# Wider rows for the loads of an attention block: V in rows of four keys with its middle keys copied on GpSimd, K in one load, output weights in row pairs

## The chip, the cores and the metric

The kernel runs on one core of a Trainium2 chip. The metric is the device time of one execution in microseconds (us). The core has a matrix engine (TensorE, "PE" in the profile, with its weight loads as "PEld"), VectorE ("DVE"), ScalarE ("ACT"), GpSimd ("POOL"), and SyncE ("SP"), which issues the DMA transfers; 16 DMA engines carry them.

## What is computed

```python
B, Sq, D = 8, 112, 640          # x:       [B, Sq, D]
H, Sk, Dh = 32, 512, 192        # k_cache, v_cache: [B, H, Sk, Dh]; wq: [D, H*Dh]; wo: [H*Dh, D]

def reference(x, k_cache, v_cache, wq, wo):
    q = (x @ wq).reshape(B, Sq, H, Dh).transpose(0, 2, 1, 3)
    scores = jnp.einsum("bhqd,bhkd->bhqk", q, k_cache) * (Dh ** -0.5)
    p = softmax(scores, axis=-1)
    o = jnp.einsum("bhqk,bhkd->bhqd", p, v_cache)
    return o.transpose(0, 2, 1, 3).reshape(B, Sq, H * Dh) @ wo
```

All inputs and the output are bf16. K and V are 50 MB each, and every byte of them is read once.

## The kernel before

**Units.** The 32 heads are cut into 8 groups of 4, and a unit is one group for one batch: 64 units, u = 8 g + b. A unit loads K and V of its four heads (768 KB each), computes the transposed scores, exponentiates them, multiplies by V, normalises, transposes the result and leaves it in `oT`. For each group, the projection of all queries (`do_Q`) and the output product (`do_O`) run as items of 128 rows or columns, handed out one to two of each per unit by the table `items_at`.

**TensorE** follows one written order (lines 883 to 893): scores of unit u (`do_S`, L840, 96 matmuls of 32 rows, four side by side), then PV of unit u-1 (`do_PV`, L856, 16 matmuls), then Q items (L803) and O items (L821) with the six transposes of unit u-1 (`do_T`, L868) between them. Group 0's queries are made before the loop from weights as they lie in memory (L810); groups 1 to 7 use weights that GpSimd has put into another order.

**Softmax sums.** No maximum is subtracted. The denominators come out of the PV product itself: each V tile has a column of ones before its first key and after its last (`vs`, columns 31 and 32 + 2 x 192 of each half), and a product reads 193 columns, one key's 192 and the ones column beside it. With four keys t = 0 to 3 in a partition the even ones read from the left, the odd ones to the right, so that a one is next to each key. Before the change each of the two halves of a tile holds two keys, with ones on both sides. The sums land in column 0 and column 193 of the product, `do_NM` on VectorE adds the two (L981) and takes the reciprocal (L984), and VectorE (L987) and ScalarE (L928) scale two heads each.

**VectorE** also turns K: `do_KT` (L976) transposes the loaded tile `kr` in 32x32 blocks of 4-byte pairs, four pieces a unit, five to eight pieces ahead of the scores. ScalarE does the exponentials (L921) and carries the queries (L913) and the transposed outputs (L938) out of PSUM.

**GpSimd** works in order, unit by unit: where the table `at` says so it reorders one 128-row piece of the next but one group's W_q (`reorder`, L1064, two copies), then it waits for the reciprocals of unit u and counts values out of range (L1079, L1080, L1082). VectorE's L980 waits for that count with a distance of three units. Ahead of the loop stand the five reorders for group 1.

**Loads.** SyncE issues all transfers from one list (from L1126), each after its own wait: K of unit u when the transposes of unit u-3 are done (`NK = 3` buffers), V of unit u when PV of unit u-4 is done (`NV = 4`), pieces of W_q when GpSimd has emptied the buffer, pieces of W_o when the group before last has been used. In the loop over u the order is K of u, V of u-1, then at most two pieces of W_q and two of W_o. K comes in two halves of 3,072-byte rows, V in two halves of 768-byte rows (two keys), W_o in pieces of 128 rows of 1,280 bytes, W_q in pieces of 1,536-byte rows. A window on the bytes in flight is in the code, but set so high that it never waits.

Of the kernel before, what the change touches and what calls it, by code (L numbers as in the profile page):

```python
# [6 lines left out]
BF16 = mybir.dt.bfloat16  # L7
F32 = mybir.dt.float32
I32 = mybir.dt.int32
# [657 lines left out]
def build_main(nc, x, k_cache, v_cache, wq, wo, out, flag):  # L667
    B, SQ, D = x.shape
# [9 lines left out]
    scale = float(DH) ** -0.5  # L678
    LO, HI = 2.0 ** -30, 2.0 ** 40
    NK, NV, NT = 3, 4, 3  # L680
    PW = 448
    RW = DH + 2
    WINDOW = 10 ** 9
    EARLY = 0
    PRE = 12
    EARLY_LOADS = ("k1", "q", "v0", "k2", "v1", "k3", "o", "v2")
    QN = (2, 2, 2)
# [26 lines left out]
    with ExitStack() as es:  # L714
# [9 lines left out]
        wqr = sb("wqr", [128, DC, 4 * DH], BF16)  # L724
        wos = sb("wos", [128, 2, 6, D], BF16)
        kr = [sb(f"kr{j}", [128, 16, DH], BF16) for j in range(NK)]
        vs = [sb(f"vs{j}", [128, 4, 2, PW], BF16) for j in range(NV)]
        kt = [sb(f"kt{j}", [128, 4, 3, 128, 2], BF16) for j in range(NT)]
        qT = [sb(f"qT{j}", [128, 6, R], BF16) for j in range(2)]
        pT = [sb(f"pT{j}", [128, 4, 4, 128], BF16) for j in range(2)]  # L730
# [18 lines left out]
        aX, aEX, aQ, aT, aNM = (sem(n) for n in ("aX", "aEX", "aQ", "aT", "aNM"))  # L749
        vI, vX, vKT, vSM, vRC, vNM, vO, vT = (sem(n) for n in ("vI", "vX", "vKT", "vSM", "vRC", "vNM", "vO", "vT"))  # L750
        gI0, gI, gB, gC, gV = (sem(n) for n in ("gI0", "gI", "gB", "gC", "gV"))
        gW = sem("gW")
        mX = [sem(f"mX{j}") for j in range(3)]
        mK = [[sem(f"mK{j}{h}") for h in range(2)] for j in range(NK)]
        mV = [[sem(f"mV{j}{h}") for h in range(2)] for j in range(NV)]
        mW0 = [sem(f"mW0{j}") for j in range(DC)]
        mWQ = [sem(f"mWQ{j}") for j in range(DC)]
        mWO = [[sem(f"mWO{j}{c}") for c in range(6)] for j in range(2)]
        mOUT = [sem(f"mOUT{j}") for j in range(MT)]
        XM = [(0, 2), (2, 4), (4, MT)]  # L760
        x_piece = [0, 0, 1, 1, 2, 2, 2]
# [20 lines left out]
        def _(pe):  # L782
# [31 lines left out]
            def do_O(it):  # L814
                _, g, m, h = it
                W(pe, aT, 8 * g + last_unit(m) + 1)
                bank_free(pe, it)
                for c in range(6):
                    if m == 0 and h == 0:
                        W(pe, mWO[g % 2][c], 16 * (g // 2 + 1))  # L820
                    mm = pe.matmul(ps[:, bank(it), 0:HO], oT[:, c, 128 * m:128 * (m + 1)],  # L821
                                   wos[:, g % 2, c, HO * h:HO * (h + 1)], start=(c == 0), stop=(c == 5))
                mm.then_inc(pO, 1)
# [20 lines left out]

            def do_PV(u):
                W(pe, aEX, 4 * (u + 1))
                for h in range(2):
                    W(pe, mV[u % NV][h], 16 * (u // NV + 1))
                W(pe, aT, u)
                W(pe, vNM, u)  # L850
                W(pe, aNM, u)
                for a in range(4):
                    for t in range(4):
                        k, e = divmod(a, 2)
                        o0, v0 = (0, 31) if t % 2 == 0 else (1, 32 + DH)
                        mm = pe.matmul(pv[:, k, e, o0:o0 + DH + 1], pT[u % 2][:, a, t, :],  # L856
                                       vs[u % NV][:, a, t // 2, v0:v0 + DH + 1], start=(t == 0), stop=(t == 3),
                                       skip_group_check=True)
                mm.then_inc(pPV, 1)

            def do_T(u):
                for j in range(6):
                    if j == 0:
                        W(pe, vNM, u + 1)
                    if j == 3:
                        W(pe, aNM, u + 1)
                    o0 = 2 * (RW * (j // 3) + 1) + SQ * (j % 3)
                    mm = pe.transpose(psb[:, 4, o0:o0 + SQ], os_[u % 2][:, 128 * j:128 * (j + 1)], ident[0:SQ, 0:SQ])  # L868
                mm.then_inc(pT_, 1)

            W(pe, gI, 1)
# [92 lines left out]
        def _(dve):  # L964
# [3 lines left out]

            def do_KT(u, t):
                if t == 0:  # L970
                    for h in range(2):
                        W(dve, mK[u % NK][h], 16 * (u // NK + 1))
                    W(dve, pS, 4 * (u - NT + 1))
                src = kr[u % NK][:, t:16:4, :].bitcast(I32).rearrange("p s (c i) -> p c s i", c=3)
                dst = kt[u % NT][:, t].rearrange("p c j e -> p c (j e)").bitcast(I32).rearrange("p c (j s) -> p c s j", s=4)
                dve.transpose(dst, src).then_inc(vKT, 1)  # L976
# [66 lines left out]
        @block.gpsimd  # L1043
        def _(gp):
            gp.memset(ident[:], 0.0).then_inc(gI0, 1)
            gp.wait_ge(gI0, 1)
            gp.affine_select(out=ident[:], in_=ident[:], compare_op=ALU.not_equal, fill=1.0, base=0,
                             pattern=[[-1, 128]], channel_multiplier=1).then_inc(gI, 1)
            for j in range(2):
                gp.memset(pT[j][:, :, :, SQ:128], 0.0)  # L1050
            for j in range(NV):
                gp.memset(vs[j][:, :, :, 31:32], 1.0)
                gp.memset(vs[j][:, :, :, 32 + 2 * DH:33 + 2 * DH], 1.0)
            gp.memset(cnt[:], 0.0).then_inc(gC, 1)
            gp.wait_ge(gC, 1)
            gp.memset(bad[:], 0.0).then_inc(gV, 1)
            gp.wait_ge(gV, 1)

            def reorder(g, dc):
                W(gp, mWQ[dc], 16 * g)  # L1060
                if dc == 0 and g >= 2:
                    W(gp, pQ, q_index[(g - 2, 5, 1)] + 1)
                for e in range(2):
                    ins = gp.tensor_copy(  # L1064
                        wqs[:, g % 2, dc, :].rearrange("p (k e a i) -> p e k a i", k=3, e=2, a=4)[:, e],
                        wqr[:, dc, :].rearrange("p (a k i e) -> p e k a i", a=4, k=3, e=2)[:, e])
                ins.then_inc(gW, 1)

            at = {}
            for g in range(1, NG):  # L1070
                for dc in range(DC):
                    at.setdefault(unit_of[(g - 2, 5, 1)] + 1 + dc if g >= 2 else -1, []).append((g, dc))
            for it in at.get(-1, []):
                reorder(*it)
            for u in range(NU):
                for it in at.get(u, []):
                    reorder(*it)
                W(gp, vRC, u + 1)
                gp.tensor_scalar(bad[:, 0, :], rinv[:, u % 4, :], LO, None, op0=ALU.is_lt)  # L1079
                gp.tensor_scalar(bad[:, 1, :], rinv[:, u % 4, :], HI, None, op0=ALU.is_gt).then_inc(gB, 1)  # L1080
                gp.wait_ge(gB, u + 1)
                gp.tensor_tensor(cnt[:], cnt[:], bad[:], op=ALU.add).then_inc(gC, 1)  # L1082
                gp.wait_ge(gC, u + 2)

        @block.sync
        def _(sp):
            loads = []

            def add(dst, src, s, count, waits):
                size = 2  # L1090
                for n in dst.shape:
                    size *= n
                loads.append((dst, src, s, count, waits, size))

            def load_x(j):
                m0, m1 = XM[j]
# [7 lines left out]
                else:  # L1104
                    add(wqr[:, dc, :], src, mWQ[dc], 16 * g, [(gW, DC * (g - 2) + dc + 1)])

            def load_wo(g, c):
                add(wos[:, g % 2, c, :], wo[4 * DH * g + 128 * c:4 * DH * g + 128 * (c + 1)], mWO[g % 2][c],
                    16 * (g // 2 + 1), [(pO, 2 * MT * (g - 1))])

            def load_k(u):
                g, b = divmod(u, B)
                src = k_cache[b, 4 * g:4 * g + 4].rearrange("a (j s) d -> (a j) (s d)", s=16)
                for h in range(2):
                    add(kr[u % NK][:].rearrange("p s d -> p (s d)")[:, 8 * DH * h:8 * DH * (h + 1)],
                        src[:, 8 * DH * h:8 * DH * (h + 1)], mK[u % NK][h], 16 * (u // NK + 1),
                        [(vKT, 4 * (u - NK + 1))])

            def load_v(u):
                g, b = divmod(u, B)  # L1120
                for h in range(2):
                    add(vs[u % NV][:, :, h, 32:32 + 2 * DH],
                        v_cache[b, 4 * g:4 * g + 4].rearrange("a (m h t) d -> h m a (t d)", h=2, t=2)[h],
                        mV[u % NV][h], 16 * (u // NV + 1), [(pPV, u - NV + 1)])

            load_x(0)  # L1126
# [5 lines left out]
            for step in EARLY_LOADS:  # L1132
# [3 lines left out]
                    for dc in range(DC):  # L1136
                        load_wq(1, dc)
                if step[0] == "o":
                    for c in range(6):
                        load_wo(0, c)  # L1140
            for u in range(4, NU + 1):
                if u < NU:
# [7 lines left out]
                for g in range(1, NG):  # L1150
                    d = u - (8 * g - 1)
                    if 0 <= d < 3:
                        load_wo(g, 2 * d)
                        load_wo(g, 2 * d + 1)
            total = 0
            ends = []
            for n, (dst, src, s, count, waits, size) in enumerate(loads):
                total += size
                ends.append(total)
                past = [i for i in range(n) if ends[i] <= total - WINDOW]  # L1160
                if past:
                    i = past[-1]
                    W(sp, loads[i][2], loads[i][3])
                for ws, wv in waits:
                    W(sp, ws, wv)
                sp.dma_start(dst, src).then_inc(s, 16)  # L1166
# [51 lines left out]
```

## Time and profile before

| | |
|---|---|
| median of 14 runs | 445.48 us (442.48 to 450.18) |
| the profiled execution | 444.12 us, of which the span from the first to the last instruction is 442.4 us |
| mean granted TensorE clock | 0.98 |
| busy: PE / DVE / ACT / POOL | 90% / 67% / 59% / 17% |
| DMA read and written | 117.5 MB and 1.15 MB, 268 GB/s over the span |
| K load, 384 KB, issue to landing | 128 of them, 5.3 us median |
| V load, 384 KB, issue to landing | 128 of them, 5.1 us median |
| W_o piece, 160 KB; W_q piece, 192 KB | 48 of them, 5.4 us; 35 of them, 5.6 us |

In the rows of the profile, a line such as "L976 DVE STREAM_TRANSPOSE kt<-kr 128x384 int32 ... x256 | 207.8, 867 | 8.4" gives the source line, the engine, the operation, what it writes and reads, the shape, how many there are, the busy time of all in us and the mean of one in ns, and after the second bar the time for which the engine stood idle just before them and what ended that. The row of a DMA queue gives packets, MB, and the share of 16 engines' span that its packets took. "Issue" is time in which an engine waited for nothing that the profile shows. The views with windows give the busy time of each engine in a stretch of time, the granted clock of TensorE, the share of the DMA engines and GB/s.

### The profile page before, as it was taken

Reading aid. Unit: us, or ns where it says so; the run is one execution under the profiler, and the core shown is the slowest. Engines: PE = TensorE matmul, PEld = TensorE weight load, DVE = VectorE, ACT = ScalarE, POOL = GpSimd, SP = SyncE. Lnnn points to the kernel's source line nnn. Section 1 sums busy time; section 2 is a strip of 40 time slices with the busy share of each in tenths; the row PEclk is TensorE's granted clock in tenths of the full one; section 3 lists DMA queues with packets and bytes.
Section 4 is the critical chain, followed back from the end, with each engine's and each line's share of the span. In section 5 each row is a group of like instructions: output and inputs, shape, how many; then the busy total and the mean of one; then the engine's idle time right before and its main releaser. Section 6 shows DMA issues by size and latency. Waiting matters only on the chain.

```text
span 442.4 us, 20613 instructions
## 1 busy us (share of the span) xinstructions
PE 397.7 (90%) x8948; PEld 299.2 (68%) x8948; DVE 297.6 (67%) x570; ACT 261.5 (59%) x549; POOL 76.8 (17%) x280
## 2 busy tenths in 40 slices
PE   7978999877999987999999899999789999988882
PEld 5556677655777765777776677777557777776661
DVE  1637877646777875877777568877648787788431
ACT  3557566644766755576665655676536766665440
POOL 1402222120122300222112201222001111111010
PEclk9989999989999999999999999999989999999898
DMA  8999999957989997799988799889857899897201
GB/s 266 368 362 337 361 362 314 310 192 221 323 257 313 313 354 224 233 286 339 337 281 257 253 347 295 246 260 319 287 162 225 257 333 314 267 309 232 73 33 37
DMA packets 100738, 120.10 MB, mean 271 GB/s; under 512 B 5664, under 2 KB 84256, under 8 KB 100640
## 3 DMA queue, kind: packets, MB, share of 16 engines
q1 hardware_dynamic: 100640, 118.71, 83.0%
q8 instruction: 72, 1.18, 1.1%
q14 instruction: 26, 0.21, 0.2%
HBM read 117.54 MB, written 1.15 MB: 268 GB/s over the span
## 4 chain that ended last, share of the span: by engine, by line
PE 88%; issue 7%; DVE 2%; DMA 1%; SPq 1%; ACT 0%; DVEq 0%
PE ps L856 22%; PE ps L821 20%; PE ps L840 19%; PE ps L803 19%; PE ps L868 5%; PE ps L810 2%; DMA wqs<-in_wq_dram 1%; DVE os L987 1%; SPq L1166 1%; DVE rinv L984 0%; DVE sm L981 0%; PE ps L789 0%; ACT oT L938 0%; DVE xT L1005 0%; DVE xs L1000 0%
## 5 line engine op out<-in xcount | busy, mean ns | idle before, releaser
L976 DVE STREAM_TRANSPOSE kt<-kr 128x384 int32<-128x384 int32 x256 | 207.8, 867 | 8.4 <-DMA kr<-in_k_cache_dram 8.4
L921 ACT ACTIVATE pT<-ps 128x448 bf16<-128x448 f32 x256 | 118.7, 548 | 78.7 <-PE ps L840 78.7
L821 PE MATMUL ps<-wos,oT 128*128 128x320 bf16 x672 | 111.8, 303 | 2.9 <-issue 1.9
L856 PE MATMUL ps<-vs,pT 128*128 128x193 bf16 x1024 | 99.7, 249 | 14.1 <-issue 13.3
L840 PE MATMUL ps<-qT,kt 32*128 32x112 bf16 x6144 | 90.2, 209 | 11.8 <-issue 11.8
L840 PEld LDWEIGHTS ps<-qT,kt 32*128 32x128 bf16 x6144 | 78.2, 93 | 31.8 <-issue 29.8
L856 PEld LDWEIGHTS ps<-vs,pT 128*128 128x128 bf16 x1024 | 84.1, 98 | 21.6 <-issue 15.9
L803 PE MATMUL ps<-xT,wqs 128*128 128x448 bf16 x420 | 94.1, 359 | 0.0
L821 PEld LDWEIGHTS ps<-wos,oT 128*128 128x128 bf16 x672 | 63.5, 99 | 31.0 <-issue 3.9
L981 DVE TENSOR_REDUCE sm<-ps 112x4 f32<-112x8 f32 x64 | 10.7, 167 | 105.3 <-PE ps L856 105.3
L913 ACT ACTIVATE qT<-ps 128x448 bf16<-128x448 f32 x96 | 52.2, 545 | 32.6 <-PE ps L803 25.0
L1079 POOL TENSOR_SCALAR bad<-rinv 112x4 f32<-112x4 f32 x64 | 14.6, 228 | 297.2 <-DVE rinv L984 296.8
L938 ACT ACTIVATE oT<-ps 128x672 bf16<-128x672 bf16 x64 | 46.7, 730 | 32.3 <-PE ps L868 32.3
L928 ACT ACTIVATE os<-ps,rinv 112x192 bf16<-112x192 f32 x128 | 46.9, 418 | 23.8 <-DVE rinv L984 21.8
L803 PEld LDWEIGHTS ps<-xT,wqs 128*128 128x128 bf16 x420 | 40.8, 99 | 28.3 <-issue 2.8
L1000 DVE TENSOR_TENSOR acc<-ps,acc 128x320 f32<-128x320 f32 x84 | 41.0, 488 | 5.2 <-PE ps L821 5.1
L1064 POOL COPY wqs<-wqr 128x384 bf16<-128x384 bf16 x70 | 33.2, 507 | 47.2 <-DMA wqr<-in_wq_dram 45.6
L987 DVE TENSOR_TENSOR os<-ps,rinv 112x384 bf16<-112x384 f32 x64 | 35.7, 558 | 6.5
L868 PE MATMUL ps<-ident,os 112*128 112x112 bf16 x384 | 30.1, 214 | 4.9 <-DVE os L987 3.1
L868 PEld LDWEIGHTS ps<-ident,os 112*128 112x128 bf16 x384 | 24.9, 98 | 13.0 <-DVE os L987 5.6
L1080 POOL TENSOR_SCALAR bad<-rinv 112x4 f32<-112x4 f32 x64 | 14.5, 226 | 4.1 <-issue 0.2
L810 PE MATMUL ps<-xT,wqs 128*32 128x448 bf16 x240 | 12.4, 353 | 1.9 <-ACT xT L904 0.9
(32 smaller groups left out, 63.3 us busy)
## 6 DMA issues: line engine op xcount, KB each, us to landing
kr<-in_k_cache_dram SPq DMA_DIRECT2D x128, 384.0 KB, 5.3
vs<-in_v_cache_dram SPq DMA_DIRECT2D x128, 384.0 KB, 5.1
wos<-in_wo_dram SPq DMA_DIRECT2D x48, 160.0 KB, 5.4
wqr<-in_wq_dram SPq DMA_DIRECT2D x35, 192.0 KB, 5.6
out_dram<-xs SPq DMA_DIRECT2D x7, 160.0 KB, 1.8
wqs<-in_wq_dram SPq DMA_DIRECT2D x5, 192.0 KB, 4.7
xs<-in_x_dram SPq DMA_DIRECT2D x2, 320.0 KB, 3.2
xs<-in_x_dram SPq DMA_DIRECT2D x1, 480.0 KB, 7.0
```

The source lines that it names most:

```text
L803: mm = pe.matmul(ps[:, bank(it), 0:HQ], wqs[:, g % 2, dc, 128 * c:128 * (c + 1)], rhs, start=(dc == 0), stop=(dc == DC - 1))
L821: mm = pe.matmul(ps[:, bank(it), 0:HO], oT[:, c, 128 * m:128 * (m + 1)], wos[:, g % 2, c, HO * h:HO * (h + 1)], start=(c == 0), stop=(c == 5))
L840: mm = pe.matmul(ps[:, a, SQ * t:SQ * (t + 1)], kt[u % NT][p, t, c // 2, :, c % 2], qT[g % 2][p, c, SQ * b:SQ * (b + 1)], start=(c == 0), ...
L856: mm = pe.matmul(pv[:, k, e, o0:o0 + DH + 1], pT[u % 2][:, a, t, :], vs[u % NV][:, a, t // 2, v0:v0 + DH + 1], start=(t == 0), stop=(t == ...
L868: mm = pe.transpose(psb[:, 4, o0:o0 + SQ], os_[u % 2][:, 128 * j:128 * (j + 1)], ident[0:SQ, 0:SQ])
L913: act.activation(qT[g % 2][:, c, HQ * h:HQ * (h + 1)], ps[:, bank(it), 0:HQ], ACTF.Copy).then_inc(aQ, 1)
L921: act.activation(pT[u % 2][:, a, :, 0:SQ], ps[:, a, 0:4 * SQ].rearrange("p (t q) -> p t q", t=4), ACTF.Exp, scale=scale).then_inc(aEX, 1)
L928: ins = act.activation(os_[u % 2][:, DH * (2 + e):DH * (3 + e)], pv[0:SQ, 1, e, 1:1 + DH], ACTF.Copy, scale=rinv[:, u % 4, 2 + e:3 + e])
L938: act.activation(oT[:, :, SQ * b:SQ * (b + 1)].rearrange("p (k c) q -> p k c q", k=2), src.rearrange("p k (c q) -> p k c q", c=3), ACTF.Co ...
L976: dve.transpose(dst, src).then_inc(vKT, 1)
L987: dve.tensor_tensor(os_[u % 2][:, 0:2 * DH].rearrange("p (e d) -> p e d", e=2), pv[0:SQ, 0, :, 1:1 + DH], rinv[:, u % 4, 0:2][:, :, None]. ...
L1000: ins = dve.tensor_tensor(ob[:, m, cs] if g == NG - 1 else acc[:, m, cs], src, acc[:, m, cs], op=ALU.add)
```

## The change

V's buffer becomes one row of four keys per head and partition: `vs` is [128, 4, 832] with the four keys at columns 32 to 799, a one at column 31 and a one at column 800. The two loads of a unit now split the heads (two each) and not the keys; each row is 1,536 bytes. The middle two keys have no ones beside them any more. GpSimd copies them into a new tile `vm` (two buffers) that holds key 1, two ones and key 2 (`middle`: two copies of 128 x 4 x 96 32-bit words a unit). PV reads keys 0 and 3 from `vs` and keys 1 and 2 from `vm`, and waits for GpSimd's count instead of the two loads' semaphores. `middle(0)` stands ahead of the reorders for group 1, `middle(1)` behind them, and `middle(u + 2)` at the end of unit u on GpSimd.

K of a unit is one load of 768 KB with 6,144-byte rows. W_o comes in three pieces a group of 256 rows, two rows (2,560 bytes) to a partition; so that the products match, the transposes of the attention output take every second column (a step of 2 in the weights that TensorE loads), and the third of the six waits for ScalarE's half where the fourth did. The window's code is taken out.

```diff
-        vs = [sb(f"vs{j}", [128, 4, 2, PW], BF16) for j in range(NV)]
+        vs = [sb(f"vs{j}", [128, 4, VW], BF16) for j in range(NV)]
+        vm = [sb(f"vm{j}", [128, 4, MW], BF16) for j in range(NM)]
...
             def do_PV(u):
                 W(pe, aEX, 4 * (u + 1))
-                for h in range(2):
-                    W(pe, mV[u % NV][h], 16 * (u // NV + 1))
+                W(pe, gM, u + 1)
...
-                        o0, v0 = (0, 31) if t % 2 == 0 else (1, 32 + DH)
-                        mm = pe.matmul(pv[:, k, e, o0:o0 + DH + 1], pT[u % 2][:, a, t, :],
-                                       vs[u % NV][:, a, t // 2, v0:v0 + DH + 1], start=(t == 0), stop=(t == 3),
-                                       skip_group_check=True)
+                        o0, src, v0 = [(0, vs[u % NV], 31), (1, vm[u % NM], 0), (0, vm[u % NM], DH + 1),
+                                       (1, vs[u % NV], 32 + 3 * DH)][t]
+                        mm = pe.matmul(pv[:, k, e, o0:o0 + DH + 1], pT[u % 2][:, a, t, :], src[:, a, v0:v0 + DH + 1],
+                                       start=(t == 0), stop=(t == 3), skip_group_check=True)
...
-                    if j == 3:
+                    if j == 2:
                         W(pe, aNM, u + 1)
                     o0 = 2 * (RW * (j // 3) + 1) + SQ * (j % 3)
-                    mm = pe.transpose(psb[:, 4, o0:o0 + SQ], os_[u % 2][:, 128 * j:128 * (j + 1)], ident[0:SQ, 0:SQ])
+                    mm = pe.transpose(psb[:, 4, o0:o0 + SQ], os_[u % 2][:, 256 * (j // 2) + j % 2:256 * (j // 2) + j % 2 + 255:2], ident[0:SQ, 0:SQ])
...
+            def middle(u):
+                for h in range(2):
+                    W(gp, mV[u % NV][h], 16 * (u // NV + 1))
+                W(gp, pPV, u - NM + 1)
+                for h in range(2):
+                    ins = gp.tensor_copy(vm[u % NM][:, :, (DH + 2) * h:(DH + 2) * h + DH].bitcast(I32),
+                                         vs[u % NV][:, :, 32 + DH * (1 + h):32 + DH * (2 + h)].bitcast(I32))
+                ins.then_inc(gM, 1)
...
+            middle(0)
             for it in at.get(-1, []):
                 reorder(*it)
+            for u in range(1, NM):
+                middle(u)
             for u in range(NU):
...
                 gp.wait_ge(gC, u + 2)
+                if u + NM < NU:
+                    middle(u + NM)
...
-            def load_wo(g, c):
-                add(wos[:, g % 2, c, :], wo[4 * DH * g + 128 * c:4 * DH * g + 128 * (c + 1)], mWO[g % 2][c],
+            def load_wo(g, k):
+                r0 = 4 * DH * g + 256 * k
+                add(wos[:, g % 2, 2 * k:2 * k + 2, :], wo[r0:r0 + 256].rearrange("(p e) d -> p e d", e=2), mWO[g % 2][k],
                     16 * (g // 2 + 1), [(pO, 2 * MT * (g - 1))])
...
-                for h in range(2):
-                    add(kr[u % NK][:].rearrange("p s d -> p (s d)")[:, 8 * DH * h:8 * DH * (h + 1)],
-                        src[:, 8 * DH * h:8 * DH * (h + 1)], mK[u % NK][h], 16 * (u // NK + 1),
-                        [(vKT, 4 * (u - NK + 1))])
+                add(kr[u % NK][:].rearrange("p s d -> p (s d)"),
+                    k_cache[b, 4 * g:4 * g + 4].rearrange("a (j s) d -> (a j) (s d)", s=16), mK[u % NK], 16 * (u // NK + 1),
+                    [(vKT, 4 * (u - NK + 1))])
...
                 for h in range(2):
-                    add(vs[u % NV][:, :, h, 32:32 + 2 * DH],
-                        v_cache[b, 4 * g:4 * g + 4].rearrange("a (m h t) d -> h m a (t d)", h=2, t=2)[h],
+                    add(vs[u % NV][:, 2 * h:2 * h + 2, 32:32 + 4 * DH],
+                        v_cache[b, 4 * g + 2 * h:4 * g + 2 * h + 2].rearrange("a (m t) d -> m a (t d)", t=4),
                         mV[u % NV][h], 16 * (u // NV + 1), [(pPV, u - NV + 1)])
```

## The prediction

> **What bounds the kernel now.** I read the page's busy shares first, then the chain that ended last, then the list of waits, and last the trace's own records of DMA packets around the places where TensorE stands still.
>
> ```profile
> PE 397.7 (90%) x8948; PEld 299.2 (68%) x8948; DVE 297.6 (67%) x570; ACT 261.5 (59%) x549; POOL 76.8 (17%) x280
> q1 hardware_dynamic: 100640, 118.71, 83.0%
> q8 instruction: 72, 1.18, 1.1%
> PE 88%; issue 7%; DVE 2%; DMA 1%; SPq 1%; ACT 0%; DVEq 0%
> ```
>
> TensorE is the bound: 88% of the chain is matmuls, none of which the change adds or removes. The DMA engines come next, 83.0% of 442.4 us = 367.3 us each. The only sizeable idle on the chain is "issue", 7% or 31 us: TensorE waits for nothing that the profile names. The list of waits of TensorE says where:
>
> ```profile
> PE ps L856 <- issue: 13.3, 9, 2.5
> PE ps L840 <- issue: 11.8, 11, 2.5
> PE ps L868 <- DVE os L987: 3.1, 7, 1.1
> ```
>
> No line names a V or K transfer: V, K and weights are in time, so a faster load pays nothing directly. But the "issue" gaps have a pattern. Number TensorE's instructions in order: every long gap lies at 193 plus a multiple of 256, and 256 instructions are one 16,384-byte packet of the instruction queue (the q8 row: 72 packets, 1.18 MB). Of 71 such crossings 26 have a gap, 30.1 us in all, and in each the refill packet started late: on average 3.8 us after the crossing before. Once it started, the next page was usable some 2.45 us later (packet at 25.46 us, TensorE on again at 27.96; at 243.01 and 245.46). The worst cases are crossings just before a V load: at 238.06 us a page began, V and a piece of W_q were issued at 238.61 to 239.59, their packets ran until about 243.0, and only then did the refill start. So **TensorE waits for its own instructions, and these wait behind the data**. A long gap costs twice, because the granted clock falls in the next 3.4 us:
>
> ```profile
> core 0: us, PE busy (x) PEld busy (x) DVE busy (x) ACT busy (x) POOL busy (x), PEclk, DMA share, GB/s
> 25.03:28.44 3.41, 0.86 (x60) 0.63 (x48) 0.00 (x0) 0.10 (x1) 0.00 (x0) 1.00 1.08 354
> 28.44:31.85 3.41, 3.41 (x25) 2.75 (x20) 0.51 (x3) 2.02 (x5) 0.00 (x0) 0.50 1.07 365
> 318.60:322.00 3.40, 0.94 (x12) 0.79 (x10) 0.57 (x1) 1.73 (x4) 0.00 (x0) 1.00 0.79 281
> 322.00:325.40 3.40, 3.40 (x16) 1.88 (x14) 1.68 (x4) 1.28 (x3) 0.65 (x3) 0.50 0.34 86
> ```
>
> Four such windows lie inside the work (from 28.4, 96.7, 322.0 and 414.2 us), each worth 1.7 us.
>
> A rule speaks against all this: the Trainium skill, "Runtime: NRT & Kernel Launch", Instruction fetch mechanics, says that crossing a 16 KiB boundary costs one step of a queue's tail and is mostly hidden. By it faster data would be worth nothing and the sum below would be zero. The trace decides: 26 of 71 crossings are not hidden.
>
> **The change, part by part.**
>
> *Rows of the loads.* Mean times of one packet in the trace's records: 768 B 40.9 ns (65,536 of them, all V), 1,280 B 59.9, 1,536 B 73.1 (W_q), 3,072 B 140.1 (16,384, all K), a semaphore write 9 ns; times their counts and over 16 engines they give the 367.3 us. After the change V is 32,768 rows of 1,536 B: 2,680 - 32,768 x 73.1 ns = 285 us less. K is 8,192 rows of 6,144 B, a size not in the trace: on the slope from 1,536 to 3,072 B (67.0 ns for 1,536 B more) it takes 140.1 + 2 x 67.0 = 274 ns, so 2,295 - 2,245 = 50 us less (nothing, if such a row is cut in two). W_o, 3,072 rows of 2,560 B at 118 ns for 6,144 at 59.9: 6 us less. 88 DMAs fewer save 1,408 semaphore writes, 13 us. Sum 354 us, over 16 engines **22.1 us, 6.0% of the DMA work**; the queue's share goes from 83% to about 78%. The Trainium skill, "DMA: Bandwidth & Descriptors", Why small descriptors are slow, gives about 3 cycles a packet beside one per 32 bytes: V's 2 x 27 cycles become 51, 5.6% of V's 167.5 us, 9.3 us, where the rows give 17.8. I take the rows; by the rule the 22.1 would be about 12.
>
> What it buys on the path: a refill that waits for data waits for 6% less of it. 26 crossings x 3.8 us x 6% = **-6.0 us** (-3.3 by the rule; 0 at the other end, if the wait is not made of data). One of the four half-clock windows, 1.7 us, may go with a gap that becomes shorter: half a chance, **-0.8 us**.
>
> *The copies on GpSimd.* Per unit two copies 128x384 int32. The nearest row is the reorder of W_q on the same engine, of as many elements:
>
> ```profile
> L1064 POOL COPY wqs<-wqr 128x384 bf16<-128x384 bf16 x70 | 33.2, 507 | 47.2 <-DMA wqr<-in_wq_dram 45.6
> ```
>
> 128 x 507 ns = 65 us, POOL at 142 us (32%). What hides it is depth: the copy for unit u+2 is made after the check of unit u, about 2 us after PV of unit u began to be normalised, and PV of u+2 comes two units, some 11 us, later. V of u+2 was issued when PV of u-2 ended and landed within 5.1 us (median). Behind it on POOL stands only the next unit's reorder, whose reader on TensorE is units away, and the check, which VectorE's L980 waits for three units later. A copy would have to take over 4 us to be seen. Nor does it hinder VectorE: its transposes (L976) that met a copy of L1064 took 876 ns, the others 865.
>
> *The start* is the exception. The copy for unit 0 stands ahead of the five reorders for group 1 and waits for V of unit 0:
>
> ```profile
> 15.20 4.56 POOL L1064 COPY wqs<-wqr 128x384 bf16<-128x384 bf16 x10 [12.72 <-DMA wqr<-in_wq_dram]
> 22.34 2.06 PE L803 MATMUL ps<-xT,wqs 128*128 128x448 bf16 x10
> 27.96 0.57 PE L840 MATMUL ps<-qT,kt 32*128 32x112 bf16 x30 [2.55 <-issue]
> ```
>
> V of unit 0 landed at 19.6 us; with shorter loads ahead say 19.1. Two copies, then 4.56 us of reorders: done at 24.7 instead of 19.8, and the Q products that began at 22.34 need them: TensorE waits 2.4 us. But 3.0 us of work later (27.7) it reaches the page end where it now waits until 27.96 for a refill asked for at 21.59, before the new wait. The new wait takes the old one's place: **0**. Without that cover it costs 2.4 us.
>
> *Queues and waits.* PV waits for one count of POOL instead of two of DMA: at most an instruction less. SP issues 88 DMAs fewer; K's second half was issued 0.4 us after the first and VectorE waited for both, so one load changes nothing there. A single K load leaves no gap for a refill to slip between halves: 0.4 us of each unit's 6, times half a K load (0.9 us), 0.06 us a page, 1.5 us over the 26; but half the gaps have V ahead, not K: **+0.5 us**, bounds 0 and +2. Piece j = 2 of the transposes L868 waits for ScalarE one piece earlier: 15 waits x 0.1 us at most, **+0.3**. Their weights are read at a stride of 2 elements: L840's loads, which do so already, take 93 ns, L868's plain ones 98: 0. PV's operands start at an odd element in two of four cases, before and after: 0. Half as many W_o rows with half the waits: 0.
>
> Sum: -6.0 - 0.8 + 0.5 + 0.3 = **-6.0 us**. The profiled execution took 444.1 us (span 442.4 and 1.7 around it), so 438.1; that execution lies 1.4 us under the median of 445.5, so the forecast for a median is **439.5 us**.
>
> **The rivals.**
>
> *Nothing moves.* The refill's wait is mostly a fixed latency: crossings at 175.6 and 412.9 us, with no data in the queue, still waited 2.1 and 2.8 us. Then only the part above 2.1 us, 1.7 of 3.8, shrinks by 6%: 26 x 0.1 = 2.7 us, against +0.8 and an exposed piece of the start: 444 to 445.5. For it also: gaps come in clusters when the page end drifts past PV, whatever the data. Against: the 4.9-us waits end exactly with V's last packets.
>
> *Slower: the refill waits behind larger rows.* If an engine takes a fixed number of data packets ahead of a refill, not a number of bytes, doubled rows double the bytes ahead. In the gap at 238 us all 64 V packets of an engine passed first, 2.6 us. If the window were some 32 packets, V's load of 32 larger rows would pass whole where today half of it does: +1.2 us at crossings that come during V. For it: in the first 70 us refills passed with 100 KB an engine still queued, after some 35 to 60 packets. Against: crossings behind K (3,072 B) waited 2.5 to 3.5 us, no more than those behind V. At ten crossings more in a gap: +12 us, less the 4 that faster data still give elsewhere: 453.5. It decides once a refill's mean wait grows past today's 3.8 us.
>
> *The start is not covered*: +2.4, maybe with one half-clock window more, +1.7: the gain shrinks to 2 us, 443.5. It belongs to the second case's range.
>
> **How the numbers follow.** Shorter waits 0.56, nothing moves 0.23, larger rows 0.21. About 0.5% (2.2 us) is what a measurement of this kernel can tell from no change. The likeliest case alone spans 435 to 443: the sum without the clock and with -3.3, and up to two half-clock windows gone. The range takes in the second case whole and half of the third: **434 to 450**. Faster: 0.56 less a small part that ends within 0.5%, plus as much from the second case: 0.57; same 0.21; slower 0.22.
>
> **What would show it.** Right: the data queue's share near 78%, with 55,200 packets (100,640 less 32,768 of V, 8,192 of K, 3,072 of W_o and 1,408 semaphore writes); "issue" in the chain 24 us or less; copies near 507 ns with POOL at 32%; no wait of L856 for POOL; a wait of about 2.4 us of L803 for POOL at 22 us. Wrong: "issue" as large as before or larger with shorter loads (the refill isn't waiting for bytes), copies well over 1 us or slower transposes on VectorE, or PV waiting for POOL.

## The result

The changed kernel takes 436.12 us (median of 10 runs, 431.87 to 437.14) against 445.39 (47 runs, 442.14 to 450.18): a ratio of 0.9775, 95% interval 0.974 to 0.9809, **9.3 us faster**. The forecast was 439.5 us. Ratios leave out executions more than 1.5% above the fastest of their kernel and medians don't, so the two can differ by some tenths of a per cent. The profiled execution, 431.81 us with a span of 429.9, is shorter than every one of the ten; that of before, 444.12 us with a span of 442.4, is near its median. The difference of the two spans, 12.5 us, therefore overstates the change.

The rows of the page of after: busy shares, the two queues, the chain by engine, VectorE's transposes of K, and the new copy.

```profile
PE 395.6 (92%) x8948; PEld 299.5 (70%) x8948; DVE 298.1 (69%) x570; ACT 261.5 (61%) x549; POOL 136.2 (32%) x410
...
q1 hardware_dynamic: 55200, 118.70, 80.8%
q8 instruction: 72, 1.18, 1.1%
...
PE 86%; issue 4%; DMA 2%; DVE 2%; SPq 2%; POOL 1%; ACT 0%; DVEq 0%; POOLq 0%
...
L976 DVE STREAM_TRANSPOSE kt<-kr 128x384 int32<-128x384 int32 x256 | 209.0, 871 | 8.2 <-DMA kr<-in_k_cache_dram 8.2
...
L1076 POOL COPY vm<-vs 128x384 int32<-128x384 int32 x128 | 61.1, 507 | 22.3 <-DMA vs<-in_v_cache_dram 18.0
```

TensorE does the same work in a shorter span. "Issue" on the chain fell from 7% of 442.4 us to 4% of 429.9. The packets are the 55,200 that were forecast, and they take 347.3 us of each DMA engine (80.8% of a shorter span; forecast 345.2). A copy takes 507 ns, as its neighbour the reorder did, and VectorE's transposes take 871 ns where they took 867.

The waits of TensorE in the same execution:

```profile
PE ps L858 <- issue: 6.8, 6, 2.1
PE ps L842 <- issue: 6.6, 7, 2.6
PE ps L805 <- POOL wqs L1066: 3.8, 1, 3.8
PE ps L869 <- DVE os L987: 3.7, 9, 1.1
```

No wait of PV (L858) for GpSimd appears, so the copies are hidden in the loop. The gaps at TensorE's page ends, every 256 instructions (below: page gaps), fell from 30.1 us in 26 places to 14.9 in 16. New is the wait of the first group-1 queries (L805) for the reorder at the start. The granted clock there:

```profile
core 0: us, PE busy (x) PEld busy (x) DVE busy (x) ACT busy (x) POOL busy (x), PEclk, DMA share, GB/s
21.20:24.60 3.40, 1.01 (x84) 0.84 (x71) 2.26 (x3) 2.16 (x5) 3.40 (x9) 0.99 1.02 400
24.60:28.00 3.40, 2.01 (x6) 0.89 (x7) 0.00 (x0) 0.00 (x0) 2.23 (x5) 0.50 1.06 392
28.00:31.40 3.40, 3.40 (x77) 2.02 (x77) 0.00 (x0) 1.09 (x2) 0.00 (x0) 0.50 1.02 382
31.40:34.80 3.40, 3.40 (x65) 2.58 (x54) 1.33 (x4) 2.84 (x7) 0.00 (x0) 1.00 0.31 111
```

TensorE stands from 22.2 to 26.0 us, and two windows at half clock follow where the kernel before had one.

### The profile page after: what moved, and what is told of

Same layout as the page of the kernel before. It is cut to its first block, busy times and chain, and to the rows that moved or that the text cites. A ratio compares the mean times of both kernels' runs of the same rounds, so it can differ in the third digit from the quotient of the medians.

```text
span 429.9 us, 20657 instructions
## 1 busy us (share of the span) xinstructions
PE 395.6 (92%) x8948; PEld 299.5 (70%) x8948; DVE 298.1 (69%) x570; ACT 261.5 (61%) x549; POOL 136.2 (32%) x410
## 3 DMA queue, kind: packets, MB, share of 16 engines
q1 hardware_dynamic: 55200, 118.70, 80.8%
## 4 chain that ended last, share of the span: by engine, by line
PE 86%; issue 4%; DMA 2%; DVE 2%; SPq 2%; POOL 1%; ACT 0%; DVEq 0%; POOLq 0%
PE ps L858 22%; PE ps L823 20%; PE ps L842 20%; PE ps L805 19%; PE ps L869 5%; DMA vs<-in_v_cache_dram 2%; SPq L1169 2%; DVE os L987 1%; POOL wqs L1066 1%; DVE rinv L984 0%; DVE sm L981 0%; POOL vm L1076 0%; ACT oT L939 0%; DVE xs L1000 0%; DVEq L767 0%
## 5 line engine op out<-in xcount | busy, mean ns | idle before, releaser
L858 PE MATMUL ps<-vs,pT 128*128 128x193 bf16 x512 | 95.8, 248 | 5.0 <-issue 5.0
L805 PE MATMUL ps<-xT,wqs 128*128 128x448 bf16 x420 | 95.1, 361 | 4.8 <-POOL wqs L1066 3.8
L1093 POOL TENSOR_SCALAR bad<-rinv 112x4 f32<-112x4 f32 x64 | 14.6, 228 | 228.6 <-DVE rinv L984 228.2
L858 PE MATMUL ps<-vm,pT 128*128 128x193 bf16 x512 | 85.2, 248 | 1.8 <-issue 1.8
L1076 POOL COPY vm<-vs 128x384 int32<-128x384 int32 x128 | 61.1, 507 | 22.3 <-DMA vs<-in_v_cache_dram 18.0
L805 PEld LDWEIGHTS ps<-xT,wqs 128*128 128x128 bf16 x420 | 40.8, 99 | 33.1 <-issue 4.1
L858 PEld LDWEIGHTS ps<-vs,pT 128*128 128x128 bf16 x512 | 47.7, 97 | 11.7 <-issue 5.8
L858 PEld LDWEIGHTS ps<-vm,pT 128*128 128x128 bf16 x512 | 46.6, 98 | 2.3 <-issue 2.3
L1000 DVE TENSOR_TENSOR acc<-ps,acc 128x320 f32<-128x320 f32 x84 | 40.9, 487 | 4.6 <-PE ps L823 4.6
L869 PE MATMUL ps<-ident,os 112*128 112x112 bf16 x384 | 30.0, 214 | 3.9 <-DVE os L987 3.7
```

What stands on the lines that cost most here:

```text
L805: mm = pe.matmul(ps[:, bank(it), 0:HQ], wqs[:, g % 2, dc, 128 * c:128 * (c + 1)], rhs, start=(dc == 0), stop=(dc == DC - 1))
L869: mm = pe.transpose(psb[:, 4, o0:o0 + SQ], os_[u % 2][:, 256 * (j // 2) + j % 2:256 * (j // 2) + j % 2 + 255:2], ident[0:SQ, 0:SQ])
L1000: ins = dve.tensor_tensor(ob[:, m, cs] if g == NG - 1 else acc[:, m, cs], src, acc[:, m, cs], op=ALU.add)
L1076: ins = gp.tensor_copy(vm[u % NM][:, :, (DH + 2) * h:(DH + 2) * h + DH].bitcast(I32), vs[u % NV][:, :, 32 + DH * (1 + h):32 + DH * (2 + h) ...
```

## The experiments

**Theory**, as predicted: TensorE's instruction refills wait behind data packets, and wider rows shorten that wait. **Rivals**: the gain comes from another part of the change, such as the one wait less that TensorE makes ahead of PV; or the refill's latency is its own and data do not matter; or larger rows lengthen the wait and something else makes up for it.

### Copies without wider rows

```diff
 # the changed kernel, with K and W_o loaded as before, and
-                    add(vs[u % NV][:, 2 * h:2 * h + 2, 32:32 + 4 * DH],
-                        v_cache[b, 4 * g + 2 * h:4 * g + 2 * h + 2].rearrange("a (m t) d -> m a (t d)", t=4),
+                    add(vs[u % NV][:, :, 32 + 2 * DH * h:32 + 2 * DH * (h + 1)],
+                        v_cache[b, 4 * g:4 * g + 4].rearrange("a (m h t) d -> h m a (t d)", h=2, t=2)[h],
```

> GpSimd copies the middle keys and PV waits for it, but V still comes in rows of two keys (768 bytes), K in halves and W_o in single rows: the same transfers as before, 63 waits fewer on TensorE. If the width of the rows made the gain (fewer packets ahead of the instruction refills), nothing is left of it: 445 to 449 us, gaps at TensorE's page ends near 30 us, and the start some 4 us later than before (a wait of the first group-1 queries for the reorder). If the gain came from the one wait less per unit on TensorE, which shifts where the page ends fall, it stays: 436 to 440 us, with the page gaps near 15 us.

Measured: 438.55 us, ratio 0.9868 (0.9807 to 0.9929). The packets are those of before:

```profile
q1 hardware_dynamic: 100640, 118.71, 83.9%
```

Yet the kernel is 6 to 7 us faster, as the second expectation had it, and the page gaps of its profile are 21.4 us, between the two expectations. More than half of the measured gain is there without one wider row. My theory had nothing for this.

### V's rows alone

```diff
 # the run above with V loaded as in the change:
+                    add(vs[u % NV][:, 2 * h:2 * h + 2, 32:32 + 4 * DH],
+                        v_cache[b, 4 * g + 2 * h:4 * g + 2 * h + 2].rearrange("a (m t) d -> m a (t d)", t=4),
```

> Only V's part of the change: copies and V rows of 1,536 bytes, K and W_o as before. V is 285 of the 354 us of packet time that the change saves, so if packet time ahead of the refills is the cause most of the gain is here: 436 to 439 us, page gaps 15 to 20 us. If K in one load or W_o in pairs made it, 443 us or more.

Measured: 434.30 us, ratio 0.9766 (0.9716 to 0.9817). That is below the 436 to 439 expected. V's wider rows take 4.3 us off the run above. The whole change has 0.9775: K in one load and W_o in pairs add nothing that shows.

### One count for V

If the copies alone are faster with the same transfers, the suspect is the wait that they replaced. The kernel before, with nothing but that:

```diff
-        mV = [[sem(f"mV{j}{h}") for h in range(2)] for j in range(NV)]
+        mV = [sem(f"mV{j}") for j in range(NV)]
...
-                for h in range(2):
-                    W(pe, mV[u % NV][h], 16 * (u // NV + 1))
+                W(pe, mV[u % NV], 32 * (u // NV + 1))
```

> The kernel before, but both halves of V count on one semaphore, so PV waits for V once instead of twice: 64 waiting instructions fewer on TensorE, every transfer and every copy as before. If the copies-only run was faster because TensorE has one instruction less per unit, so that its page ends fall elsewhere against the loads, this run is faster too, by as much or more since the start is not delayed: 435 to 440 us, page gaps 17 to 24 us. If the copies themselves did it, nothing changes: 445 us and 30 us of gaps.

Measured: 438.36 us, ratio 0.9872 (0.9814 to 0.993). No copies, no wider rows, and the same gain as the copies-only run: a wait on a semaphore can be an instruction of its own on TensorE, and its records hold 317 of them instead of 380. Its page gaps are 25.2 us, just over the range expected. What is missing from them stands near the end. The "issue" waits of TensorE's matmuls there, from 360 us on, first in the kernel before (to 432 us), then in this run (to 425 us):

```profile
PE ps L856 <- issue: 2.5, 2, 1.8
PE ps L868 <- issue: 0.8, 1, 0.8
PE ps L821 <- issue: 0.8, 1, 0.8
PE ps L840 <- issue: 0.2, 1, 0.2
...
PE ps L855 <- issue: 0.2, 1, 0.2
```

### The wait put back

```diff
 # the changed kernel
+                W(pe, mV[u % NV][0], 16 * (u // NV + 1))
                 W(pe, gM, u + 1)
```

> The changed kernel with one more wait per unit ahead of PV, on a semaphore that was reached long before: TensorE has as many instructions as the kernel before again. If their number sets where the page ends fall, some 5 to 8 us come back: 441 to 444 us, page gaps 25 us or more. If it doesn't, 436 us.

Measured: 440.17 us, ratio 0.9889 (0.9831 to 0.9948), just below the range expected; 4.1 us of the changed kernel's gain are gone again. The waits of TensorE in its profile:

```profile
PE ps L859 <- issue: 11.9, 9, 2.6
PE ps L842 <- issue: 10.8, 11, 2.4
PE ps L870 <- DVE os L988: 3.1, 7, 1.1
PE ps L805 <- POOL wqs L1067: 2.4, 1, 2.4
```

The added wait is for a semaphore reached long before, and no line shows TensorE waiting for it. What grew is "issue", from 6.8 and 6.6 us to 11.9 and 10.8: the page gaps are 27.6 us.

### Without V's loads

```diff
 # the kernel before
-                for h in range(2):
+                for h in range(2 if u < NV else 0):
                     add(vs[u % NV][:, :, h, 32:32 + 2 * DH],
...
-                    W(pe, mV[u % NV][h], 16 * (u // NV + 1))
+                    W(pe, mV[u % NV][h], 16)
```

> The kernel before, with V's loads left out after the first four units (PV then reads old V, and the output differs): 47 of the 118 MB less in the queue. If the refills wait behind data, the page gaps fall from 30 us to below 8 and the span to about 415 us. If they wait for a latency of their own and for where the page ends fall, the gaps stay above 20 us and the span above 430 us.

Measured, one run: 419.34 us, span 417.6. It lies between the two expectations, nearer to the first.

```profile
q1 hardware_dynamic: 37280, 71.51, 53.5%
...
PE 91%; issue 3%; DVE 2%; DMA 1%; SPq 1%; ACT 0%; DVEq 0%
```

The page gaps are 12.4 us, in 15 places, where they were 30.1. So most of the gaps is V's data ahead of the refills, but some 40% of them stays with the queue busy only half of the time. The wait of a refill shrinks less: on average it starts 2.9 us after the crossing before it in the kernel before, and 2.3 us here.

### The start

```diff
-            middle(0)
             for it in at.get(-1, []):
                 reorder(*it)
-            for u in range(1, NM):
+            for u in range(NM):
                 middle(u)
```

> The whole change, with the copy for unit 0 behind the five reorders instead of ahead of them. If the wait of 3.8 us for the reorder and the half-clock window behind it are lost time, as the profile after says, the run is 3 to 5 us faster than the changed kernel: 431 to 433 us. If the refill of the same page would be waited for in any case, as the prediction argued, there is no gain: 436 us.

Measured: 434.22 us, ratio 0.9733 (0.967 to 0.9795), 1.9 us under the changed kernel, with intervals that overlap. It lies between the expectations. With V's rows alone the same edit was run too:

> Only V's part of the change, with the copy for unit 0 behind the reorders. The V-rows-only run took 434.3 us and the start was worth 1.9 us in the whole change: 431 to 433 us if the two add up; 434 if the refill of that page waits anyway.

Measured: 433.21 us, ratio 0.9733 (0.9678 to 0.9788), 1.1 us under the run without it. Twice the same sign and about the size that the two timelines give (unit 2's scores began at 33.72 us before and at 35.48 after, 1.8 us later), but neither alone is more than its uncertainty.

### Fewer waits still

PV also waits for the normalisation of unit u-1 on VectorE and on ScalarE. TensorE has waited for both already, ahead of the transposes that stand before PV in its own order. In the run above they are taken out:

```diff
                 W(pe, aT, u)
-                W(pe, vNM, u)
-                W(pe, aNM, u)
```

> As the run before it, without the two waits ahead of PV that TensorE has already made ahead of the transposes of the unit before: 126 waiting instructions fewer again. If each wait costs time of its own (about 0.1 us), the run gains 10 us or more: 421 us. If the number matters only through where page ends fall, it can go either way by a few us, and the page gaps go with it: 426 to 440 us, time less page gaps unchanged.

Measured: 428.96 us, ratio 0.966 (0.9604 to 0.9716). TensorE's records hold 63 waits fewer, not 126: where a wait can ride on the instruction behind it, it is no instruction of its own. So the 421 us of the first expectation becomes some 427, and the time alone does not tell a cost of each wait from a shift of the page ends. The profile says more: of 8.9 us between the two spans, 4.0 are page gaps and 3.4 two windows of half clock less; 1.5 us are neither. This is the fastest kernel of the study, 16 us under the kernel before, and its interval lies wholly below that of the changed kernel.

### The page ends moved

```diff
 # the kernel before, ahead of the first queries
+            for j in range(64):
+                pe.matmul(ps[:, 7, 0:32], ident[:], ident[:, 0:32], start=True, stop=True)
```

> The kernel before with 64 small matmuls, 128 instructions, more on TensorE ahead of the first queries: half a page, the number per unit unchanged. If the gaps come in clusters wherever the page end passes the V load, and the instructions per unit set only how often that is, every cluster moves by half of its period (about 37 us): near 50, 125, 200, 275 and 350 us instead of 88, 162, 238, 308 and 391, the sixth falls behind the last loads, and the page gaps fall from 30 to 20 to 26 us although there are more instructions: 438 to 443 us. If every instruction or wait costs time of its own, nothing falls, and the added work makes it slower: 446 us or more.

Measured: 443.88 us (14 runs), ratio 0.9923 (0.9879 to 0.9966). The clusters moved as expected: gaps at 47 to 72, 134 to 154, 207 to 222, 282 to 294 and 358 to 378 us, where the kernel before has them at 88 to 105, 163 to 176, 238 to 256, 309 to 330 and 391 to 413. But there are five of them here too, none fell off the end, and the page gaps of the profiled execution (450.3 us, one of the longest of the 14) are 32.6 us, not 20 to 26. The time lies between the two expectations. The run shows that the clusters move with the number of instructions ahead of them. It does not tell what an instruction or a wait costs: the added ones are matmuls, take 1.7 us once, and stand where TensorE had partly been waiting.

### K in one load, on the best kernel

```diff
 # the fastest kernel above
-                for h in range(2):
-                    add(kr[u % NK][:].rearrange("p s d -> p (s d)")[:, 8 * DH * h:8 * DH * (h + 1)],
-                        src[:, 8 * DH * h:8 * DH * (h + 1)], mK[u % NK][h], 16 * (u // NK + 1),
+                add(kr[u % NK][:].rearrange("p s d -> p (s d)"),
+                    k_cache[b, 4 * g:4 * g + 4].rearrange("a (j s) d -> (a j) (s d)", s=16), mK[u % NK], 16 * (u // NK + 1),
```

> The V-rows run with the early copy moved and the double waits taken out, with K in one load of 6,144-byte rows in addition. By the packet times K saves 50 of 5,600 us of packets and takes away a place for a refill between the halves: 427 to 431 us, no difference that can be told from 429. If larger rows ahead of a refill lengthen its wait, as the rival had it, 433 us or more, with a longer mean wait of the refills.

Measured: 431.26 us, ratio 0.966 (0.9592 to 0.9728), the same ratio as without; the median is 2.3 us longer. The mean wait of a refill in its profile is 2.8 us against 2.5. No gain from K's larger rows, and no loss that can be told from zero.

### V's rows again, at the smaller number of instructions

```diff
 # the kernel before with one count for V, and
-                W(pe, vNM, u)
-                W(pe, aNM, u)
```

> The kernel before with V on one semaphore and without the two double waits: TensorE has the same instructions per unit as the V-rows run without them, which took 429.0 us, but V comes in rows of two keys and GpSimd copies nothing. If the row's width is worth what the prediction gave for V (285 of 354 us of packets, 4.8 us on the path), this takes 433 to 435 us. If all of the gain was the instructions, 429 us; if the rows made all of it, 440 us.

Measured: 435.79 us, ratio 0.979 (0.9733 to 0.9847). That is just above the 433 to 435 expected. Three waits a unit taken out of the old kernel, with no new tile, copy or row, give the changed kernel's time. Against the fastest kernel, which has the same waits on TensorE, the narrow rows cost 6.8 us by the medians and 1.3% by the ratios. A third pair with equal waits on TensorE is on record, from one session: one count for V (438.36 us, 0.9814 to 0.993) against V's rows with the start moved (433.21 us, 0.9678 to 0.9788), 5.2 us. With the 4.3 us of the first pair, V's rows are worth 4 to 7 us.

## Why the prediction was right, and where it was wrong

Every profiled execution adds up in one way. Take from the span the page gaps, 1.7 us for each half-clock window inside the work (3.41 us at 0.50), and the wait for the reorder at the start:

| kernel | waits in TensorE's records | span | page gaps | half-clock windows | wait at the start | rest |
|---|---|---|---|---|---|---|
| before | 380 | 442.4 | 30.1 | 4 | 0 | 405.5 |
| after | 317 | 429.9 | 14.9 | 4 | 3.8 | 404.4 |
| copies only | 317 | 435.6 | 21.4 | 4 | 2.8 | 404.6 |
| V rows only | 317 | 429.3 | 20.1 | 1 | 2.3 | 405.2 |
| one count for V | 317 | 435.6 | 25.2 | 3 | 0 | 405.3 |
| after, extra wait | 380 | 438.3 | 27.6 | 1 | 2.4 | 406.6 |
| after, start moved | 317 | 433.7 | 22.8 | 3 | 0 | 405.8 |
| V rows, start moved | 317 | 431.6 | 23.2 | 2 | 0 | 405.0 |
| the same, fewer waits | 254 | 422.7 | 19.2 | 0 | 0 | 403.5 |
| old rows, fewer waits | 254 | 433.4 | 24.4 | 3 | 0 | 403.9 |
| K in one load, on the best | 254 | 430.4 | 22.1 | 2 | 0 | 404.9 |
| page ends moved | 380 | 448.3 | 32.6 | 6 | 0 | 405.5 |
| without V's loads | 380 | 417.6 | 12.4 | 1 | 0 | 403.5 |

The rest is the same to 3 us while the spans differ by 31. So the reading of the bound holds: a kernel whose matmuls are fixed, that loses its time at TensorE's page ends and in the clock windows behind them. These are single executions; what is faster is told by the medians and ratios.

**The packet sum was right, and its value on the path near.** A 1,536-byte row took 74.3 ns (73.1 assumed), a 6,144-byte row 276.7 (274 extrapolated), a 2,560-byte row 107.6 (118); 20.1 us less per engine where 22.1 were forecast. For V alone the step would have given 6.0 x 285 / 354 = 4.8 us, and the three pairs gave 4.3, 5.2 and 6.8. By the fixed cost per packet in the Trainium skill, "DMA: Bandwidth & Descriptors", Why small descriptors are slow, two rows made into one save 5.6%, an estimate of 2.5 us; the packets here show 9% (74.3 ns for 2 x 40.9). The first pair does not rule the 2.5 us out, the others speak for the packet rows. (Redone for all rows, the prediction's "about 12" by that rule is nearer 13.) K and W_o, together 56 of the 354, were to give 1 us; in three pairs of kernels, the last with K alone, the ratios agree to 0.001 and the medians are 1.0 to 2.3 us longer, so nothing was gained.

Only a part of V's gain took the way that the forecast gave it, 26 refills that wait 6% less. In the three pairs the mean wait of all refills fell by 0.02, 0.08 and 0.15 us of 2.6, where 6% is 0.16, and the page gaps by 1.3, 2.0 and 5.2 us. Another part came through the clock: its mean over all executions rose from 0.979 to 0.984, from 0.978 to 0.983 and from 0.985 to 0.988, which is 2.3, 2.4 and 1.3 us of full clock.

**The step that failed is "at most an instruction less".** PV's wait for one count instead of two was costed at nothing, without a reason. It is the largest term: 6 us in the run that changes nothing else, 4 to 5 us back when it is added again. With the wait put back, the kernel is the one that the forecast had summed: 440.17 us, and 439.5 were forecast. The mechanism is the one the prediction had named, page ends against loads, but I had applied it to the data only. A unit has on average 276.6 instructions on TensorE and a page 256, so from unit to unit the page end slides by 20.6; every 12 units or so, 75 us, it passes the place where the refill comes just behind V. With one instruction less it slides by 19.6, and the period in the profiles is about 80 us: clusters at 88, 160, 247 and 329 us in the changed kernel, and no fifth one before the loads end near 400. The fifth, at 391 us in the kernel before with 4.7 us of gaps, is back at 389 us in the run with the extra wait. In sum, the profiles of before and of one count for V differ by this cluster alone: their page gaps up to 380 us are 24.8 and 25.2 us; 5.3 us of later gaps and the half-clock window at 414 us are in the first only, 7.0 us, and the spans differ by 6.8.

That the number of waits changes the gaps and the time is shown; that it does so through the number of clusters is what these two profiles and the places of the clusters fit. It is not the whole of it. With the extra wait the earlier clusters are larger than in the changed kernel too, and that was not taken apart. And the rest in the table falls by about 1 us for 63 waits less (some 406, 405 and 404 us on average, without the run that lacks V's loads), so some of the gain may be time of the waits themselves.

**The start was covered only in part.** The wait was forecast at 2.4 us and hidden behind a refill. It was 3.8 us (the copy for unit 0 began at 20.5 us, where V of unit 0 was assumed at 19.1). The refill's gap of 2.55 us at 28 us is indeed gone, so TensorE stood 1.2 us longer, with a second half-clock window behind. The rows show 1.8 us lost, the two runs 1.9 and 1.1.

**No half-clock window less.** The profile after has four inside the work, as before: two at the start where there was one, and one less in the loop. The granted clock of all executions has a median of 0.981 before and 0.982 after, so nothing of the -0.8 us can be told from zero. Such a window hangs on little. In the kernel before, TensorE was idle for 2.55, 2.31, 2.46 and 1.89 us in the 3.41 us ahead of the four; three such stretches with 1.62, 1.60 and 1.99 us idle had none behind them. The last of these holds most of the 2.44 us gap that ended at 245.5 us; its beginning fell into the stretch before, and it cost no clock.

**The copies** cost what their row said, 507 ns, and are hidden. The +0.3 us of the transposes isn't seen: L869 waits 3.7 us for VectorE where it waited 3.1, but so it does in the copies-only run with the old transposes, and with the extra wait it is 3.1 again.

So the forecast of a gain of 6 us was right in its sign and near in what it had summed, and short of the measured 9.3: roughly 6 from the missing wait, which was left out, 4 to 5 from V's rows, about as forecast, and 1 to 2 lost at the start. The 6 us came on top by luck; nothing in the prediction says that an instruction less would help.

**Nothing moves** falls as an outcome, with the runs without V's loads and with V's rows; its premise, that most of a refill's wait is no data, stands for V's data, since 2.3 of 2.9 us stay without V's loads. **Larger rows** falls for V: with equal waits on TensorE a refill waits no longer behind the wider rows (2.94 and 2.90 us for before and the changed kernel with the extra wait; 2.56 and 2.54, 2.57 and 2.49, 2.64 and 2.49 in the three pairs). The 2.5 us of the changed kernel itself, against 2.9, goes with the waits and not with the rows, for one count for V has 2.6. K's single load on the best kernel shows a longer wait, without an effect on the time that can be told from zero.

## What to carry to other kernels

Where an engine runs thousands of instructions without a loop and the profile shows "issue" gaps, number its instructions: here all long gaps stood at one place in every 256, and both the packets ahead of the refills and the number of waits per unit changed how much time they took. Take out waits that the engine's own order has already made, before rebuilding any transfer; here three waits a unit less were worth as much as the whole change, and V's rows of double width came on top. A step put ahead of others on a helper engine is costed by who waits for what stands behind it, the clock included.

## What the runs showed that was not expected

A wait on a semaphore that was reached long before is not free on TensorE: in four pairs of kernels 63 of them moved the median by 3 to 6 us, each time up with more waits, though the profiles show TensorE waiting at none of them. The Trainium skill, "Runtime: NRT & Kernel Launch", Instruction fetch mechanics, calls the crossing of a 16 KiB boundary mostly hidden; in every profile here 15 or more of some 70 crossings were not, and even without V's loads they cost 12.4 us.
